# Holding eight output stores behind later loads in a fused retention and feed-forward kernel

## The chip, the cores and the metric

The kernel runs on one core of a Trainium2 chip. The metric is the device time of one execution in microseconds; smaller is better. The core has five engines with instruction queues of their own: TensorE (PE in the profile; PEld is its loading of weights), VectorE (DVE), ScalarE (ACT), GpSimd (POOL, called Pool here) and SyncE (SP). SyncE computes nothing here: it issues DMA transfers, in the order of its queue. An instruction that waits holds up everything behind it on its engine. The transfers themselves run on 16 DMA engines that all queues share.

## The reference

For 8 batches and 8 heads, with 576 positions and a head dimension of 64, retention is computed, and its output, as a matrix `x` of 4608 tokens by 512, goes through a feed-forward layer with a cosine gate:

```python
scores = scale * np.matmul(q, k.transpose(0, 1, 3, 2))
gamma = 1.0 - 2.0 ** (-5.0 - np.arange(H, dtype=np.float32))
Dmat = np.where(rel >= 0, gamma[:, None, None] ** rel[None, :, :], 0.0)
ret = scores * Dmat[None, :, :, :]
attn_out = np.matmul(ret, v)
x = attn_out.transpose(0, 2, 1, 3).reshape(B * S, H * D)

h = x @ w_in            # 512 x 2048
g = h * np.cos(h)
out = g @ w_out         # 2048 x 512
```

Inputs and output are float32; the kernel's matmuls take bfloat16.

## The kernel before

**Two tilings.** Retention works on 36 blocks of 128 tokens (`g` in the code). The feed-forward layer works on tiles of tokens (`n`): tile 0 has 512 tokens, tiles 1 and 2 have 256 each, and tiles 3 to 9 have 512 each. The output is counted in row blocks `s` of 128 rows; tiles 0 to 2 make row blocks 0 to 7, and tile 3 begins with row block 8.

**A block's way.** `load` (line 105) issues from SyncE three DMAs for a block, `fq`, `fk` and `fv`, each into a tile of a pool with five buffers for each name. `prep` (line 131) scales q and k into `qks` and casts v into `vb`, on Pool for nearly all blocks (lines 140 and 156). `transposes` (line 164) turns `qks` into `qkT`: for blocks from 6 on this is a DMA with transpose, again on SyncE (line 167). Then TensorE computes the scores (`sc`, line 195), VectorE masks them into `ret` (line 207), and `attn_out` (line 293) makes the block's part of the tile's `xT`.

**A tile's way.** `mm1` (line 354) multiplies `xT` by `w_in` into `h`; ScalarE computes the cosine (line 373) and VectorE the gated product `gT` (line 374). What follows differs:

- Tiles 0 to 2 use `mm2` (line 376): for each row block 16 matmuls (line 382) into one PSUM tile, a copy by ScalarE into a tile `ot` (line 392), a store from SyncE (line 393), and then `feed(s)`.
- Tiles 3 to 9 use `mm2_seven` (line 527), Strassen's scheme with seven products (line 517) in the order 3, 4, 5, 2, 1, 7, 6. Sums of parts of `gT` that the products need, `gs`, are made by VectorE and Pool (line 445); Pool makes them in pieces of 2 x 256 = 512 elements per partition, before the change and after it. Product 3 goes into a PSUM tile, and ScalarE copies it into `u22` (line 557). Product 5 then adds into the same PSUM tile, and its copy is `c12` (line 564). In the same way product 4 and product 2 share a tile, with the copy `c21` (line 569). VectorE joins the rest into `u11` and `u22` (lines 559 and 537). The four results `c12`, `c21`, `u11` and `u22` are stored by `store` (line 542), each store followed by `feed`.

**What sets the order.** The order of each engine's instructions is the order in which the Python code emits them. `feed(s)` (line 599) is called with each finished row block and emits, as far as limits counted in `s` allow, further `prep`s, transposes and `load`s. In `feed`, after row block 7, loads up to block 19 have been emitted, all of them behind the stores of the row blocks before them in SyncE's queue.

**Buffers of the output tiles.** All results, `ot` of tiles 0 to 2 and the four of the later tiles, come from one pool, `op` (line 70), with two buffers for each of its tags "a", "b", "c" and "d". Row block `s` takes tag `"oabcd"[1 + s % 4]`, so row blocks 0 to 3 and 4 to 7 fill all eight buffers. `u22` takes tag "a", `u11` "b", `c12` "c" and `c21` "d". A tile that takes a used buffer waits until the store that reads that buffer is complete; the waits are put in by the framework.

Of the kernel before, what the change touches and what calls it, by code (L numbers as in the profile page):

```python
# [17 lines left out]
def kernel(  # L18
# [38 lines left out]
    S7 = 3  # L57
# [106 lines left out]
    def transposes(g, banks=None, only=(0, 1)):  # L164
        qks, vb, qkT, qT = tiles["a", g]
        if g >= N_PE_T:
            nc.sync.dma_start(qkT, qks.rearrange("s m h d -> s (m h d)"), transpose=True)  # L167
            return
        for m in only:
            ps = psum.tile([P, HG, P], BF16, tag=banks[m], name="tr")  # L170
            for hg in range(HG):
                nc.tensor.transpose(
                    ps[:, hg, :],
                    qks[:, m, 2 * hg : 2 * hg + 2, :].rearrange("s h d -> s (h d)"),
                    ident,
                )
            nc.scalar.copy(qkT[:, m * HG : (m + 1) * HG, :], ps)
        if ("fv", g) in tiles and g != 3:
            nc.scalar.copy(vb, tiles.pop(("fv", g)))
# [196 lines left out]
    def mm2(n, tsi, et):  # L376
        gT = tiles["g", n]
        if et == 0:
            bank = {0: "nmnm", 1: "nm", 2: "mn"}[n][tsi]
            tiles["o", tsi] = psum.tile([P, DM], F32, tag=bank, name="o")  # L380
        ps = tiles["o", tsi]
        nc.tensor.matmul(  # L382
            ps,
            lhsT=gT[:, et, tsi * P : (tsi + 1) * P],
            rhs=w_out_sb[:, et, :],
            start=(et == 0),
            stop=(et == ET - 1),
        )
        if et == ET - 1:
            s = starts[n] // P + tsi  # L390
            ot = op.tile([P, DM], F32, tag="oabcd"[1 + s % 4], name="ot")
            nc.scalar.copy(ot, ps)  # L392
            nc.sync.dma_start(out[s * P : (s + 1) * P, :], ot)
            feed(s)

    E2 = ET // 2
    N2 = DM // 2
# [93 lines left out]
    def product(n, x):  # L491

        gT = tiles["g", n]
        parts = [(j, 0, N2) for j in range(2)]
        if x in (3, 4, 7) or (x == 1 and n < last):
            ps = psum.tile([P, 2, N2], F32, tag={3: "n", 4: "st", 1: "n", 7: "st"}[x], name="o")
            tiles["o", x] = [ps[:, j] for j in range(2)]
            tiles["all", x] = ps
        elif x == 1:
            ps = psum.tile([P, N2], F32, tag="n", name="o")  # L500
            pt = psum.tile([P, 2, 512], F32, tag="a", name="o")
            tiles["o", x] = [ps] + [pt[:, k, : N2 // 2] for k in range(2)]
        if x in (1, 6) and n == last:
            parts = [(0, 0, N2), (1, 0, N2 // 2), (1, N2 // 2, N2)]
        dst = tiles["o", {5: 3, 2: 4, 6: 1}.get(x, x)]
        lhs = {3: gT[:, :E2, :256], 4: gT[:, E2:, 256:]}.get(x)
        if lhs is None:
            lhs = tiles["gs", n, x]
        rhs = {5: w_quarter(1, 1), 2: w_quarter(0, 0)}.get(x)
        if rhs is None:  # L510
            rhs = w_sum[x]
        order = [(e, i) for e in range(E2) for i in range(len(parts))]
        if len(parts) > 2:
            order.sort(key=lambda u: u[1])
        for e, i in order:
            j, c0, c1 = parts[i]
            nc.tensor.matmul(  # L517
                dst[i],
                lhsT=lhs[:, e, j * P : (j + 1) * P],
                rhs=rhs[:, e, c0:c1],  # L520
                start=(x in (3, 4, 1, 7) and e == 0 and (i == 0 or len(parts) > 2)),
                stop=(e == E2 - 1 and (i == len(parts) - 1 or len(parts) > 2)),
                skip_group_check=True,
            )
        return parts

    def mm2_seven(n, at):

        s0 = starts[n] // P
        pend = []  # L530

        def flush():
            while pend:
                pend.pop(0)()

        def add(out_, in0, in1, op_=ALU.add):
            pend.append(lambda: nc.vector.tensor_tensor(out=out_, in0=in0, in1=in1, op=op_))  # L537

        def new(tag):
            return op.tile([P, 2, N2], F32, tag=tag, name="ot")  # L540

        def store(t, r, c, s):
            r0 = starts[n] + r * 256
            nc.sync.dma_start(
                out[r0 : r0 + 256, c * N2 : (c + 1) * N2].rearrange("(j p) c -> p j c", p=P), t
            )
            feed(s)

        for x in (3, 4, 5, 2, 1, 7, 6):
            if x in at:  # L550
                at[x](flush, pend)
            else:
                flush()
            parts = product(n, x)
            if x == 3:
                u22 = new("a")
                nc.scalar.copy(u22, tiles["all", 3])
            elif x == 4:
                pend.insert(0, lambda: nc.vector.tensor_tensor(
                    out=u22, in0=tiles["all", 4], in1=u22, op=ALU.add  # L560
                ))
            elif x == 5:
                c12, u11 = new("c"), new("b")
                nc.scalar.copy(c12, tiles["all", 3])  # L564
                add(u11, u22, tiles["all", 3], ALU.subtract)
                store(c12, 0, 1, s0)
            elif x == 2:
                c21 = new("d")
                nc.scalar.copy(c21, tiles["all", 4])  # L569
                add(u22, u22, tiles["all", 4], ALU.subtract)  # L570
                store(c21, 1, 0, s0 + 1)
            elif x == 1 and n < last:
                add(u11, tiles["all", 1], u11)
            elif x == 1:
                for (j, c0, c1), ps in zip(parts, tiles["o", 1]):
                    add(u11[:, j, c0:c1], ps, u11[:, j, c0:c1])
            elif x == 7:
                add(u11, tiles["all", 7], u11)
                flush()
                store(u11, 0, 0, s0 + 2)  # L580
            elif n < last:
                add(u22, tiles["all", 1], u22)
                flush()
                store(u22, 1, 1, s0 + 3)
            else:
                for (j, c0, c1), ps in zip(parts, tiles["o", 1]):
                    add(u22[:, j, c0:c1], ps, u22[:, j, c0:c1])
                    flush()
                    r0 = starts[n] + 256 + j * P
                    nc.sync.dma_start(out[r0 : r0 + P, N2 + c0 : N2 + c1], u22[:, j, c0:c1])  # L590
# [3 lines left out]
    def prep_next(**kw):  # L594
        nonlocal prepared
        prep(prepared, **kw)
        prepared += 1

    def feed(s):

        nonlocal loaded, prepared, transposed
        before = loaded
        n, r = divmod(s - starts[S7] // P, 4)
        if n >= 0:
            while prepared < min(NG, starts[S7] // P + 10 + 4 * n + ((0, 1, 2, 4) if n else (-1, 0, 1, 4))[r]):
                prep_next()
            while transposed < prepared:
                transposes(transposed)
                transposed += 1
            ahead = starts[S7] // P + 14 if n == 0 and r < 3 else prepared + LD  # L610
            while loaded < min(NG, prepared + LD, ahead):
                load(loaded)
                loaded += 1
            return
        while True:
            while prepared < min(loaded, 2 * s + 7, s + 11, starts[S7] // P + 8):
                prep(prepared)
                prepared += 1
                if transposed < N_PE_T:
                    transposed += 1  # L620

            if N_PE_T <= transposed < min(prepared, s + 11) and (
                transposed <= loaded - 2 or loaded == NG or (s > 3 and loaded == before)
            ):
                transposes(transposed)
                transposed += 1
            elif loaded < min(NG, 2 * s + 8, s + 13):
                load(loaded)
                loaded += 1
            else:  # L630
                break
# [148 lines left out]
    for n, w in enumerate(widths):  # L780
# [68 lines left out]
        for i, (tsi, et) in enumerate(order):  # L849
            while todo and todo[0][0] <= i:  # L850
                todo.pop(0)[1]()
            mm2(n, tsi, et)
# [31 lines left out]
```

## Time and profile before

| what | us |
|---|---|
| median of three runs (least, greatest) | 300.19 (299.92, 301.33) |
| the profiled execution's own time | 299.92 |
| its span, first to last instruction | 298.2 |
| TensorE busy | 287.1 |
| Pool busy | 209.4 |
| VectorE busy | 207.9 |
| ScalarE busy | 135.9 |
| store to landing, least / median / greatest | 1.6 / 3.6 / 5.8 |

The span is divided by the profile into what each engine did. TensorE is busy for 96% of it. The DMA engines are busy for nine tenths or more of nearly every slice up to 210 us, at some 200 GB/s, most of it in packets of under 512 bytes, which are the rows of 64 floats of q, k and v. Tile 0's first matmuls of `mm1` start at 17.9 us, tile 1's at 49.2, tile 2's at 67.5, tile 3's at 84.2, tile 4's at 116.8 and tile 5's at 149.8. The eight stores of line 393 are issued by SyncE at 41.04, 51.44, 62.31, 72.91, 84.74, 96.66, 105.38 and 109.62 us. The copies that fill them were made by ScalarE between 39.0 and 85.0 us.

A line of the timeline gives start and length in microseconds, the engine (SPq is the part of SyncE that issues DMAs), the line of the code, the operation, what is written and read, and how many are merged into the line. Brackets give the idle time before it and what ended that.

### The profile page before, as it was taken

How to read it: one execution, taken by the hardware profiler on the slowest of the kernel's cores; microseconds unless marked ns; L12 is line 12 of the kernel's file. 1: busy time of each engine (PE TensorE's matmuls, PEld its weight loads, DVE VectorE, ACT ScalarE, POOL GpSimd, SP SyncE). 2: the span in 40 equal slices, each digit the busy share in tenths (PEclk: the TensorE clock that was granted, in tenths of full speed). 3: DMA queues.
4: the chain of work that ended last, by engine and by line, in shares of the span. 5: the costliest groups of instructions: out<-in, count | busy, mean ns of one | idle time of the engine just before them, and what ended most of it. 6: DMA issues, size and time to landing. Idle time of an engine off the chain costs nothing.

```text
span 298.2 us, 7384 instructions
## 1 busy us (share of the span) xinstructions
PE 287.1 (96%) x3113; PEld 195.3 (65%) x3113; DVE 207.9 (70%) x245; ACT 135.9 (46%) x167; POOL 209.4 (70%) x214
## 2 busy tenths in 40 slices
PE   8899999999999999979999999999999999999995
PEld 3478646848578786448744875488448845874584
DVE  5677637564579994788848874887489757935872
ACT  2656433514255432642346554546464446425620
POOL 2750066436445599997999999599959946980693
PEclk9999999999999999999999999999999999999999
DMA  7999999999999999999999997998690260031013
GB/s 203 212 209 206 209 214 213 200 243 208 208 174 222 211 239 213 217 279 176 198 224 229 209 200 183 212 208 201 122 194 2 73 143 0 2 106 36 0 44 99
DMA packets 154304, 50.28 MB, mean 169 GB/s; under 512 B 140832, under 2 KB 153248, under 8 KB 154272
## 3 DMA queue, kind: packets, MB, share of 16 engines
q1 hardware_dynamic: 149504, 45.10, 77.2%
q0 software_dynamic: 4224, 4.19, 8.5%
q8 instruction: 24, 0.39, 0.6%
q10 hardware_dynamic: 544, 0.52, 0.5%
q14 instruction: 8, 0.07, 0.1%
HBM read 36.70 MB, written 9.44 MB: 155 GB/s over the span
## 4 chain that ended last, share of the span: by engine, by line
PE 43%; POOL 25%; SPq 13%; DMA 8%; DVE 5%; issue 3%; ACT 1%; POOLq 0%; DVEq 0%
PE h L365 22%; POOL gs L445 17%; PE o L517 11%; SPq L117 8%; POOL qks L140 6%; PE o L382 5%; SPq L167 4%; DVE gT L374 3%; DMA fk<-in_k_dram 2%; DMA w_in_sb<-in_moe_w_in_dram 2%; DMA qkT<-qks 2%; POOL vb L156 2%; DVE gs L445 2%; DMA fv<-in_v_dram 1%; ACT cosh L373 1%
## 5 line engine op out<-in xcount | busy, mean ns | idle before, releaser
L445 POOL TENSOR_TENSOR gs<-gT 128x512 bf16<-128x512 bf16 x102 | 116.3, 1180 | 29.4 <-DVE gs L445 29.4
L365 PE MATMUL h<-xT,w_in_sb 128*128 128x512 bf16 (+2 forms) x832 | 127.6, 313 | 2.6 <-DVE gT L374 1.8
L374 DVE TENSOR_TENSOR gT<-h,cosh 128x1024 bf16<-128x1024 f32 x72 | 87.8, 1223 | 43.7 <-ACT cosh L373 40.7
L373 ACT ACTIVATE cosh<-h,half_pi 128x1024 f32<-128x1024 f32 x72 | 80.2, 1114 | 72.2 <-PE h L365 69.8
L365 PEld LDWEIGHTS <-w_in_sb 128*128 128x128 bf16 x832 | 75.9, 98 | 51.6 <-issue 3.0
L140 POOL TENSOR_TENSOR qks<-fq,gq 128x512 bf16<-128x512 f32 x32 | 34.0, 1062 | 40.9 <-DMA fq<-in_q_dram 40.9
L517 PEld LDWEIGHTS <-gs 128*128 128x128 bf16 x576 | 53.6, 98 | 10.1 <-POOL gs L445 2.9
L140 POOL TENSOR_TENSOR qks<-fk,gk 128x512 bf16<-128x512 f32 x35 | 37.3, 1066 | 8.0 <-DMA fk<-in_k_dram 7.4
L207 DVE TENSOR_TENSOR ret<-sc,tri 128x1024 bf16<-128x1024 f32 x32 | 38.1, 1217 | 2.8 <-PE sc L195 2.7
L517 PE MATMUL o<-ws,gs 128*128 128x256 bf16 (+1 forms) x352 | 39.1, 268 | 0.7 <-POOL gs L445 0.5
L382 PE MATMUL o<-w_out_sb,gT 128*128 128x512 bf16 x128 | 30.1, 380 | 0.0
L517 PE MATMUL o<-w_out_sb,gT 128*128 128x256 bf16 x224 | 26.6, 273 | 0.1
L517 PE MATMUL o<-w_out_sb,gs 128*128 128x256 bf16 x224 | 26.1, 273 | 0.5 <-POOL gs L445 0.4
L537 DVE TENSOR_TENSOR ot<-o,ot 128x512 f32<-128x512 f32 (+2 forms) x25 | 14.9, 603 | 14.7 <-PE o L517 14.5
L517 PEld LDWEIGHTS <-gT 128*128 128x128 bf16 x224 | 21.4, 98 | 4.7 <-DVE gT L374 0.7
L350 ACT CAST xT<-ov 128x1024 bf16<-128x1024 f32 (+1 forms) x18 | 16.5, 917 | 16.1 <-PE ov L319 13.9
L445 DVE TENSOR_TENSOR gs<-gT 128x1024 bf16<-128x1024 bf16 (+1 forms) x18 | 20.4, 1148 | 0.3
L382 PEld LDWEIGHTS <-gT 128*128 128x128 bf16 x128 | 11.8, 98 | 12.5
L156 POOL CAST vb<-fv 128x512 bf16<-128x512 f32 x22 | 14.3, 651 | 4.4 <-DMA fv<-in_v_dram 4.2
L564 ACT COPY ot<-o 128x512 f32<-128x512 f32 x7 | 4.1, 586 | 20.5 <-PE o L517 20.5
L392 ACT COPY ot<-o 128x512 f32<-128x512 f32 x8 | 4.7, 588 | 17.4 <-PE o L382 17.4
L537 DVE TENSOR_TENSOR ot<-ot,o 128x512 f32<-128x512 f32 x14 | 9.6, 684 | 4.0 <-ACT ot L569 2.4
(70 smaller groups left out, 175.8 us busy)
## 6 DMA issues: line engine op xcount, KB each, us to landing
out_dram<-ot SPq DMA_DIRECT2D x35, 256.0 KB, 4.0
fk<-in_k_dram SPq DMA_DIRECT2D x32, 256.0 KB, 5.2
fv<-in_v_dram SPq DMA_DIRECT2D x32, 256.0 KB, 5.2
fq<-in_q_dram SPq DMA_DIRECT2D x30, 256.0 KB, 4.5
w_in_sb<-in_moe_w_in_dram POOLq DMA_DIRECT2D x4, 512.0 KB, 8.9
w_out_sb<-in_moe_w_out_dram POOLq DMA_DIRECT2D x4, 512.0 KB, 16.2
fq<-in_q_dram SPq DMA_DIRECT2D x8, 128.0 KB, 4.0
fk<-in_k_dram SPq DMA_DIRECT2D x8, 128.0 KB, 4.4
```

Of the source, the lines that this page charges most:

```text
L117: i = nc.sync.dma_start(f[p0:p1], src[b, :, s0 : s0 + p1 - p0, :].rearrange("h s d -> s h d"))
L140: eng.tensor_tensor(out=qks[:, m].rearrange("p (b a) d -> p a b d", a=2), in0=f.rearrange("p (a b) d -> p a b d", a=2), in1=by[:, c, :].re ...
L156: copy_v(vb, fv)
L207: nc.vector.tensor_tensor(out=ret.rearrange("p a b i -> p (a b) i"), in0=ps.rearrange("p a b i -> p (a b) i"), in1=mask.unsqueeze(1).to_br ...
L350: evac(tiles["x", n][:, :, t0 : t0 + len(gs) * P], ps.rearrange("p c x i -> p c (x i)"))
L365: nc.tensor.matmul(ps[:, j, :], lhsT=w_in_sb[:, dg, (et + j) * P : (et + j + 1) * P], rhs=xT[:, dg, c0 : c0 + w], start=(dg == 0), stop=(d ...
L373: nc.scalar.activation(cosh, ps, ACTF.Sin, bias=half_pi, scale=1.0)
L374: nc.vector.tensor_mul(gT[:, et : et + m, c0 : c0 + w], ps, cosh)
L382: nc.tensor.matmul(ps, lhsT=gT[:, et, tsi * P : (tsi + 1) * P], rhs=w_out_sb[:, et, :], start=(et == 0), stop=(et == ET - 1),)
L445: i = (nc.vector if on_dve else nc.gpsimd).tensor_tensor(out=tiles["gs", n, x][:, e : e + step], in0=i0, in1=i1, op=op_)
L517: nc.tensor.matmul(dst[i], lhsT=lhs[:, e, j * P : (j + 1) * P], rhs=rhs[:, e, c0:c1], start=(x in (3, 4, 1, 7) and e == 0 and (i == 0 or l ...
L537: pend.append(lambda: nc.vector.tensor_tensor(out=out_, in0=in0, in1=in1, op=op_))
```

## The change

In tiles 0 to 2 the store is no longer issued with its row block: the row block's tile is put on a list, `held`. After the `feed` of row block 7, behind all loads that this call and earlier ones emitted, the stores of row blocks 0 to 3 are issued. The stores of row blocks 4 to 7 follow one by one, each behind the `feed` that follows one of tile 3's four stores. The number of stores and their bytes are the same, and nothing is computed differently.

```diff
@@ mm2 @@
             s = starts[n] // P + tsi
             ot = op.tile([P, DM], F32, tag="oabcd"[1 + s % 4], name="ot")
             nc.scalar.copy(ot, ps)
+            held.append((s, ot))
+            feed(s)
+            if s == 7:
+                store_held(4)
+
+    held = []
+
+    def store_held(k):
+        for s, ot in held[:k]:
             nc.sync.dma_start(out[s * P : (s + 1) * P, :], ot)
-            feed(s)
+        del held[:k]
@@ mm2_seven, store @@
                 out[r0 : r0 + 256, c * N2 : (c + 1) * N2].rearrange("(j p) c -> p j c", p=P), t
             )
             feed(s)
+            if n == S7:
+                store_held(1)
```

## The prediction

> **What bounds the kernel now.** I read the page's busy row first (TensorE busy 96% of the span), then the timeline of TensorE over 48 to 180 us, then the timelines of ScalarE and of SyncE's DMA queue over the same time. The busy row says that the end moves only if TensorE is made to wait or stops waiting. These TensorE lines (start, length, line, operation, count; in brackets the idle time before and what ended it) are the passage that the change can reach:
>
> ```profile
> 99.55 4.12 PE L517 MATMUL o<-w_out_sb,gT 128*128 128x256 bf16 x32
> 103.59 0.64 PE L195 MATMUL sc<-qkT 64*64 64x128 bf16 x32
> 104.17 3.67 PE L517 MATMUL o<-w_out_sb,gs 128*128 128x256 bf16 x32
> ...
> 108.28 0.32 PE L266 MATMUL st<-v_odd,qks 128*64 128x64 bf16 x8 [0.45 <-POOL gs L445]
> ...
> 130.81 1.89 PE L365 MATMUL h<-xT,w_in_sb 128*128 128x512 bf16 x8 [1.78 <-DVE gT L374]
> ```
>
> The first line is products 3 and 4 of tile 3, the second the scores of blocks 12 and 13, the third products 5 and 2. There is no gap between them, so every microsecond by which product 5 starts after 104.17 is a microsecond of TensorE. Behind it two gaps, 0.45 and 1.78 us, could be given back. What product 5 needs is on ScalarE:
>
> ```profile
> 101.49 0.59 ACT L557 COPY ot<-o 128x512 f32<-128x512 f32 x1 [0.58 <-PE o L517]
> 106.12 0.59 ACT L564 COPY ot<-o 128x512 f32<-128x512 f32 x1 [4.05 <-PE o L517]
> ```
>
> The first is the copy of product 3 into `u22`. Product 5 adds into the same PSUM tile, so it can't begin before this copy has read it. Now the SyncE queue, which issues in order:
>
> ```profile
> 41.04 1.13 SPq L393 DMA_DIRECT2D out_dram<-ot  x1
> 42.22 0.43 SPq L117 DMA_DIRECT2D fq<-in_q_dram  x1
> ...
> 84.74 0.57 SPq L393 DMA_DIRECT2D out_dram<-ot  x1
> 86.39 1.47 SPq L167 DMA_TRANSPOSE qkT<-qks  x1
> ...
> 96.66 0.53 SPq L393 DMA_DIRECT2D out_dram<-ot  x1
> 98.04 1.25 SPq L167 DMA_TRANSPOSE qkT<-qks  x1
> ...
> 105.38 1.08 SPq L393 DMA_DIRECT2D out_dram<-ot  x1
> 106.50 0.43 SPq L117 DMA_DIRECT2D fq<-in_q_dram  x1
> ...
> 109.62 0.89 SPq L393 DMA_DIRECT2D out_dram<-ot  x1
> 110.56 0.43 SPq L117 DMA_DIRECT2D fq<-in_q_dram  x1
> 111.03 2.27 SPq L117 DMA_DIRECT2D fk<-in_k_dram  x1
> 113.35 1.61 SPq L117 DMA_DIRECT2D fv<-in_v_dram  x1
> 115.06 0.88 SPq L544 DMA_DIRECT2D out_dram<-ot  x1
> ```
>
> The reader is to see how late SyncE runs. Row block 7 was copied by ScalarE at 84.38, and its store is issued at 109.62; tile 2's last load, block 19, is issued at 113.35 to 114.96, and tile 3's first store at 115.06. TensorE is by then 11 us into tile 3's products. From 31.8 to 115 us the queue has hardly a hole, and the page's second part shows DMA at 9 in every slice of it.
>
> **What the Trainium skill says.** "Perfetto Trace Analysis", What "DMA-bound" means: an issuing queue that is solid DMA slices is itself a bound. The trace agrees, with the gaps above (1.08 us ahead of 86.39, 0.85 ahead of 98.04) where a transpose waits for Pool instead. "TensorE: Matmul & The Clock Gate", Part 1: after an idle window of about 3.4 us the array runs at half rate until about 3.4 us of activity have passed. The trace shows the slow start only at the program's beginning: the 14 warm-up matmuls of 128x512 take 5.32 us, 380 ns each, against 13.98 us for 64 such ones at 149.83, 218 ns each; the granted clock reads 1.00 in both. "SBUF — State Buffer", Who interferes with whom: a VectorE instruction with two SBUF inputs and a GpSimd instruction that reads SBUF exclude each other. The trace agrees: the VectorE sum of 128x1024 at 126.30 takes 3.33 us while Pool works without a break, and 0.69 us at 135.14; behind it stands the 1.78 us gap.
>
> **The change part by part.**
>
> *Eight stores leave the load stream.* Each removed store gives SyncE back the time to the next issue: 1.18 us for row block 0 (41.04 to 42.22), 0.58 each for 1, 2 and 3 (the same reading at 51.44, 62.31, 72.91), 1.12 for 6, 0.94 for 7. Blocks 4 and 5 give nothing there, because the transpose behind them waits for Pool's scaling anyway. The sum is 1.18 + 3 x 0.58 + 1.12 + 0.94 = 5.0 us. Counted in DMA time it is the same: between 258 and 262 us one store runs alone with a DMA share of 0.19 over 4 us, 0.76 us; eight are 6.1 us, and since the shares in this stretch add up to 1.24 they are worth about 4.9 us of it. What do earlier loads buy? TensorE's only gap before 103 us in this stretch, 0.69 us at 67.49, waits for VectorE's `xT` copy, not for a load. So this part is worth nothing at the end by itself (bounds: 0 to 0.5 us gain; I take 0).
>
> *Four stores behind tile 2's loads.* They take the place where tile 3's first store stood, 115.06, less the 5.0 us: row block 0 is issued at about 110.1. Bounds: 107.5 if all eight count fully and landings quicken too, 112 if the waits for Pool eat most of it. A store's landing takes 1.6, 3.6 or 5.8 us (least, median, most of all stores); behind a full queue of loads I take 4.2. It lands at 114.3.
>
> *The new wait.* `u22` of tile 3 is the third tile of tag "a", which has two buffers; in the changed program it gets row block 0's, and the copy at L557 waits for that store. In the kernel before, that store was issued at 41.04 and cost nothing; now it lands at 114.3, and the copy, wanted at 101.49, ends at 114.3 + 0.59 = 114.9. With about 0.1 us to TensorE, product 5 starts at 115.0 instead of 104.17: 10.8 us of standing still. Queued behind the copy on ScalarE are the copies of `c12` and `c21` and the next `xT`; on VectorE the sum L559, which needs `u22`, with the masks of blocks 12 and 13 behind it. All of these feed TensorE work later than product 5, and keep their distance to it. Row blocks 1, 2 and 3 land up to some 3 us after block 0; `c12`, which waits for block 2, is wanted 2 us after product 5's start, so this stays about level. Bounds of the stall: 107.5 + 3.6 + 0.7 - 104.2 = 7.6 us and 112 + 5.8 + 0.7 - 104.2 = 14.3 us.
>
> *Half rate after the stall.* The trace of before has no long idle time of TensorE in its middle, so this is bounded: 0, or half of 3.4 us up to all of it if the window is met badly. An estimate from the skill's clock page: 3.4 us at half rate lose 1.7 us. I take 1.7 (0 to 3.4).
>
> *What is given back.* The 0.45 us gap is put down to Pool's sums (104.76 to 111.46), which will be done by then; it may rather be VectorE's sum at 107.47 to 108.14, which frees the PSUM bank that the next matmuls write, and VectorE, 0.43 us behind TensorE at L559 before, starts level with it after the stall. In either reading the gap goes. Pool's scaling of blocks 17 to 21 (116.25 to 129.07) depends on loads 20 and 21, which SyncE may issue only after tile 3's first store; that store waits for `c12`, ready about 117.7 instead of being issued at 115.06. Loads 20 and 21 come some 3 us later than before, Pool is free by about 131, and VectorE's sum comes at 126.30 + 10 = 136 without Pool beside it: the 1.78 us gap goes. The later gaps (0.46, 0.27 and 0.40 us at 147, 149 and 172) follow TensorE's own pace and stay. Given back: 2.2 us (0 to 3.4).
>
> *Four stores with tile 3's.* One each behind its four stores, 0.5 to 1.1 us of SyncE each, in a stretch where loads for tile 5 follow. Pool needs those from 149 us on, now about 159, so 3 to 4 us of delay are covered; if that cover of 6 us were gone, each microsecond would show. Row block 7's store comes only behind loads 22 to 26, at about 156. Tile 4's `d` tile does not wait for it: in the changed program's waits it takes the buffer of tile 3's `c21`, stored at about 126. Cost 0.
>
> *Sum.* 10.8 + 1.7 - 2.2 = +10.3 us. From 180 to 249 us TensorE runs without gaps at 29.4 us per tile, so nothing more comes back. The profiled execution took 299.92 us (span 298.2 and 1.7 around it): 310.2. The median of the runs is 300.19, 0.27 higher: **310.5 us**.
>
> **The rivals.**
>
> *A short stall (0.17).* The stream gains as much as the lower bound says, with quick landings: 7.6 us, no half rate, 3.4 us given back: +4.2, 304.4 us. For it: DMA-saturated slices; against: the waits for Pool at 86.39 and 98.04.
>
> *A second wait (0.14).* SyncE stands from about 113 to 117.7 for `c12`, and loads 20 to 22 slip by more than the 6 us of cover, so Pool's sums of tile 4 come late: 6 to 8 us on top, about 317. For it: Pool is busy almost without holes from 104 to 185 us; against: its waits there are for VectorE, not for loads.
>
> *No stall, not slower (0.05).* Loads, Pool and transposes form a chain in which one waits for the other; if each removed store shortened it by more than its own time, row block 0 would land before product 5 wants it. That takes an issue by about 100 us, so 15 us gained, 1.9 us per store against the 0.62 counted here. From there on the time is 299.9 to 300.2, or up to 2 us less if the gaps close too. That the copy doesn't wait at all, because `u22` takes another buffer, would end the same way; the changed program's waits speak against it.
>
> **How the numbers follow.** The likeliest case holds 0.64: 310.5 us, its own range 307 to 314.5. Down to 305 takes in most of the short stall, up to 316 part of the second wait: 305 to 316 leaves out about 2 in 10. 0.5% (1.5 us) is about what a measurement can tell from no change. Slower: 0.64 + 0.17 + 0.14 = 0.95; the last case splits into same 0.03 and faster 0.02.
>
> **What would show it.** In the changed profile: ScalarE's copy of `u22` waits about 12 us, ended by the DMA out_dram; TensorE has one gap of about 11 us ahead of the products of `gs` near 104; the first matmuls after it take up to twice their 115 ns for 128x256; the four stores stand together near 110 to 113 in SyncE's queue; no gap ahead of tile 4's last h matmuls. I am wrong if the four stores are issued before 101 us, or if a gap of some microseconds stands anywhere else after 130 us.

## The result and the profile after

The changed kernel takes 311.24 us (310.99 to 312.31, four runs) against 300.06 us for the kernel before on the same chip: ratio 1.0371, 95% interval 1.0332 to 1.0411. The forecast was 310.5 us. The profiled execution has a span of 309.3 us, 11.1 more than before.

In the view of all waits, the new one has these lines (who waited for whom: us in total, times, longest):

```profile
ACT ot L568 <- DMA out_dram<-ot: 15.5, 1, 15.5
...
PE o L526 <- ACT ot L568: 12.7, 1, 12.7
DVE ot L570 <- ACT ot L568: 12.5, 1, 12.5
```

One wait of ScalarE for a store, 15.5 us long, and behind it one wait each of TensorE and VectorE for ScalarE. No other line of this view is a wait for a store (`out_dram<-ot`). In the timelines of SyncE's DMA queue, of ScalarE and of TensorE the same wait has its place:

```profile
110.52 1.15 SPq L117 DMA_DIRECT2D fv<-in_v_dram  x1
111.72 2.61 SPq L402 DMA_DIRECT2D out_dram<-ot  x4
120.68 0.38 SPq L553 DMA_DIRECT2D out_dram<-ot  x1
```

```profile
99.54 1.12 ACT L373 ACTIVATE cosh<-h,half_pi 128x1024 f32<-128x1024 f32 x1 [0.69 <-PE h L365]
116.15 0.59 ACT L568 COPY ot<-o 128x512 f32<-128x512 f32 x1 [15.49 <-DMA out_dram<-ot]
120.06 0.59 ACT L575 COPY ot<-o 128x512 f32<-128x512 f32 x1 [3.33 <-PE o L526]
```

```profile
99.34 4.19 PE L526 MATMUL o<-w_out_sb,gT 128*128 128x256 bf16 x32
103.46 0.64 PE L195 MATMUL sc<-qkT 64*64 64x128 bf16 x32
116.78 4.99 PE L526 MATMUL o<-w_out_sb,gs 128*128 128x256 bf16 x32 [12.69 <-ACT ot L568]
121.70 0.32 PE L266 MATMUL st<-v_odd,qks 128*64 128x64 bf16 x8
...
129.80 13.98 PE L365 MATMUL h<-xT,w_in_sb 128*128 128x512 bf16 x64
143.61 3.66 PE L526 MATMUL o<-w_out_sb,gT 128*128 128x256 bf16 x32
...
160.46 0.61 PE L526 MATMUL o<-ws,gs 128*128 128x256 bf16 x4 [0.27 <-POOL gs L454]
```

SyncE issues the four held stores from 111.72 us, straight behind block 19's last load. The copy into `u22`, now on line 568, starts at 116.15, when the first of them has landed; before, it started at 101.49. Product 5 starts at 116.78 instead of 104.17. SyncE then stands until the copy of `c12` is made, and issues its store at 120.68. The lines from 143.61 us on show what was given back: no gap stands in front of tile 4's products, and the small gap before 160.46 is the one that the kernel before has here:

```profile
149.38 0.61 PE L517 MATMUL o<-ws,gs 128*128 128x256 bf16 x4 [0.27 <-POOL gs L445]
```

The view of stretches gives TensorE's granted clock (the column behind POOL's count) after the stall; its columns are the stretch, its length, busy time and count of PE, PEld, DVE, ACT and POOL, the clock, the DMA share and GB/s:

```profile
105.00:110.00 5.00, 0.00 (x0) 0.00 (x0) 0.00 (x0) 0.00 (x0) 5.00 (x6) 0.93 1.29 220
110.00:115.00 5.00, 0.00 (x0) 0.00 (x0) 0.00 (x0) 0.00 (x0) 5.00 (x6) 0.50 1.31 231
115.00:118.00 3.00, 1.22 (x6) 0.86 (x6) 1.23 (x2) 0.59 (x1) 3.00 (x4) 0.50 0.75 289
118.00:120.00 2.00, 2.00 (x14) 1.51 (x12) 1.72 (x2) 0.00 (x0) 2.00 (x3) 0.61 0.00 0
120.00:125.00 5.00, 5.00 (x113) 4.29 (x111) 3.46 (x6) 2.79 (x5) 3.50 (x5) 1.00 0.81 100
```

The clock falls to 0.50 while TensorE stands and is back at 1.00 in the stretch from 120 us. Products 5 and 2 run in between: 4.99 us, against 3.67 before.

The shift of TensorE against the kernel before, read from these lines and those of before:

| event | before | after | shift |
|---|---|---|---|
| product 5 starts | 104.17 | 116.78 | 12.61 |
| tile 4's h begins | 116.78 | 129.80 | 13.02 |
| tile 4's products begin | 132.53 | 143.61 | 11.08 |
| tile 5's h begins | 149.83 | 160.91 | 11.08 |
| span | 298.2 | 309.3 | 11.1 |

So 12.61 us of later start, and 4.99 - 3.67 = 1.32 us of half rate, make 13.93. Up to tile 4's h 0.91 us of that is gained back (13.93 - 13.02), and 1.94 within tile 4, where the gap of 1.78 us is gone. What is left, 11.08 us, stays to the end.

### The profile page after: what moved, and what is told of

Its sections match the earlier page's. It is cut to its first block, busy times and chain, and to the rows that moved or that the text cites. A ratio compares the mean times of both kernels' runs of the same rounds, so it can differ in the third digit from the quotient of the medians.

```text
span 309.3 us, 7382 instructions
## 1 busy us (share of the span) xinstructions
PE 288.3 (93%) x3113; PEld 196.2 (63%) x3113; DVE 205.6 (66%) x245; ACT 135.8 (44%) x167; POOL 209.4 (68%) x214
## 4 chain that ended last, share of the span: by engine, by line
PE 48%; POOL 28%; DMA 9%; SPq 7%; issue 4%; DVE 1%; POOLq 0%; ACT 0%; DVEq 0%
PE h L365 24%; POOL gs L454 19%; PE o L526 11%; PE o L382 7%; POOL qks L140 7%; SPq L117 6%; DMA fk<-in_k_dram 4%; DMA fq<-in_q_dram 4%; PE sc L195 2%; DMA fv<-in_v_dram 1%; POOL vb L156 1%; PE ov L333 1%; PE ov L319 1%; SPq L167 1%; PE st L266 1%
## 5 line engine op out<-in xcount | busy, mean ns | idle before, releaser
L526 PEld LDWEIGHTS <-gs 128*128 128x128 bf16 x576 | 54.4, 99 | 23.1 <-issue 13.0
L526 PE MATMUL o<-w_out_sb,gs 128*128 128x256 bf16 x224 | 27.4, 281 | 13.2 <-ACT ot L568 12.7
L454 DVE TENSOR_TENSOR gs<-gT 128x1024 bf16<-128x1024 bf16 (+1 forms) x18 | 17.0, 957 | 0.3
L570 DVE TENSOR_TENSOR ot<-o,ot 128x512 f32<-128x512 f32 x7 | 4.8, 685 | 13.3 <-ACT ot L568 12.5
L575 ACT COPY ot<-o 128x512 f32<-128x512 f32 x7 | 4.1, 586 | 19.8 <-PE o L526 19.8
```

The lines of the kernel that those rows point to most:

```text
L454: i = (nc.vector if on_dve else nc.gpsimd).tensor_tensor(out=tiles["gs", n, x][:, e : e + step], in0=i0, in1=i1, op=op_)
L526: nc.tensor.matmul(dst[i], lhsT=lhs[:, e, j * P : (j + 1) * P], rhs=rhs[:, e, c0:c1], start=(x in (3, 4, 1, 7) and e == 0 and (i == 0 or l ...
```

## The experiments

**Is it the wait for the store's landing, or SyncE's queue?** Four kernels, e1 to e4, ask this; the kernel before ran beside them at 299.95 us. In e1 the held stores are left out:

```diff
-            nc.sync.dma_start(out[s * P : (s + 1) * P, :], ot)
+            pass
```

> The changed kernel with the eight held stores left out: row blocks 0 to 7 of the output are never written, so this run shows what the load stream does without these stores and what tile 3 does without a store to wait for. Theory (the time is lost by the copy into u22, which waits for row block 0's store): no stall at product 5, 299.9 us, within 0.7 of the kernel before; block 19's last load still ends near 111.7 us as in the changed kernel, because the loads gain little. Rival (the loss comes from TensorE's stall alone, but earlier loads are worth something that the stall hides): 297 to 298.5 us. Rival (the loss comes from SyncE's queue, in which loads 20 and 21 stand behind the held stores): near 300 us too, so this run doesn't tell it apart; the next three do.

Measured: 299.65 us, ratio 0.9988 (0.9976 to 0.9999). Product 5 starts at 103.92, without a gap, and the copy into `u22` waits only for TensorE:

```profile
103.92 3.67 PE L526 MATMUL o<-w_out_sb,gs 128*128 128x256 bf16 x32
```

```profile
101.45 0.59 ACT L568 COPY ot<-o 128x512 f32<-128x512 f32 x1 [0.63 <-PE o L526]
```

Block 19's last load ends its issue at 110.04, 4.9 us earlier than in the kernel before; it was expected at 111.7. The medians differ by 0.3 us: earlier loads alone buy next to nothing.

The next two, e2 and e3, move the four stores forward in SyncE's queue by one and by two blocks' loads (in e3 the condition is `s == 6`):

```diff
-            feed(s)
             if s == 7:
                 store_held(4)
+            feed(s)
```

> Stores of row blocks 0 to 3 issued ahead of row block 7's feed, so that block 19's three loads stand behind them instead of before them; all else as in the changed kernel. Theory: row block 0's store is issued at about 108.0 instead of 111.7 us, lands near 112.3, product 5 starts near 113.1: the stall shrinks from 12.7 to 9.0 us and the time from 311.2 to 307.5 us. Rival (SyncE's queue and the loads behind it): block 19 to 21 are loaded later, not earlier, so 311 to 312 us.

> The same, with the four stores ahead of row block 6's feed: the loads of blocks 18 and 19 stand behind them. Theory: issue at about 104.5, landing near 108.8, product 5 near 109.6: stall 5.5 us, 304.0 us, a little less if TensorE comes back before it falls to half rate. Rival (SyncE's queue): 311 to 313 us.

Measured: 307.93 us (ratio 1.0256, 1.022 to 1.0292) and 303.69 us (1.0119, 1.0081 to 1.0157). The TensorE line of product 5 in each:

```profile
113.47 5.48 PE L526 MATMUL o<-w_out_sb,gs 128*128 128x256 bf16 x32 [9.20 <-ACT ot L568]
```

```profile
109.84 5.05 PE L526 MATMUL o<-w_out_sb,gs 128*128 128x256 bf16 x32 [5.56 <-ACT ot L568]
```

Here the store's place in the queue is the dose and the stall the response:

| kernel | store of row block 0 issued | copy into u22 starts | product 5 starts | TensorE stood | time |
|---|---|---|---|---|---|
| two loads earlier | 104.72 | 109.20 | 109.84 | 5.56 | 303.69 |
| one load earlier | 108.25 | 112.83 | 113.47 | 9.20 | 307.93 |
| as changed | 111.72 | 116.15 | 116.78 | 12.69 | 311.24 |

From the issue of the store to product 5 it takes 5.1 to 5.2 us in all three, and each microsecond of earlier issue is about a microsecond of time. The loads of blocks 18 and 19 are later in the two experiments than in the changed kernel; if they had set the time, it would have risen. Loads 20 and 21 come earlier, not later as the rival had it: load 20 is issued at 119.52 and 117.12 us instead of 122.50, because tile 3's first store, which waits for `c12`, stands ahead of it and `c12` is ready sooner. But in e3 it is issued even before that of the kernel before (118.13), and the time is still 3.7 us longer. The rival on SyncE's queue falls.

In e4, row block 0 is stored at once and only 1 to 7 are held:

```diff
             held.append((s, ot))
+            if s == 0:
+                store_held(1)
             feed(s)
             if s == 7:
-                store_held(4)
+                store_held(3)
```

> Only row block 0 is stored at once, as before; row blocks 1 to 7 are held as in the changed kernel. Theory: u22 gets its buffer in time and product 5 starts at 104.2, but the copy into c12 waits for row block 2's store, which lands near 116.5, and the next matmuls that use its PSUM bank start near 117.9 instead of 108.3: a stall of 9.6 us in a new place, with half rate behind it, and 309 us. Rival (it is row block 0's store alone): 300 to 301 us. Rival (SyncE's queue): 311 us.

Measured: 309.04 us, ratio 1.0302 (1.0276 to 1.0327). TensorE and ScalarE:

```profile
103.51 3.67 PE L528 MATMUL o<-w_out_sb,gs 128*128 128x256 bf16 x32
118.02 0.43 PE L266 MATMUL st<-v_odd,qks 128*64 128x64 bf16 x8 [10.83 <-DVE ot L548]
```

```profile
101.16 0.59 ACT L570 COPY ot<-o 128x512 f32<-128x512 f32 x1 [0.63 <-PE o L528]
116.56 0.58 ACT L577 COPY ot<-o 128x512 f32<-128x512 f32 x1 [14.82 <-DMA out_dram<-ot]
```

Product 5 is on time, at 103.51. The copy of `c12` waits for row block 2's store, and the next matmuls into its PSUM bank start after a gap of 10.83 us. The wait isn't the first store's own: take it away, and the next tile that needs a held store's buffer stops TensorE 3 us later, at 107.18 instead of 104.10.

**The four stores that go with tile 3's.** In e5 only row blocks 4 to 7 are held; the kernel before ran beside it at 299.92 us:

```diff
             held.append((s, ot))
+            if s < 4:
+                store_held(1)
             feed(s)
-            if s == 7:
-                store_held(4)
```

> Row blocks 0 to 3 are stored at once, as before; only row blocks 4 to 7 are held, one behind each store of tile 3. Theory (a held store costs only where a tile of tile 3 waits for it, and these four are first waited for in tiles 4 and 5, long after they land): no stall, within 0.7 us of the kernel before, 299.3 to 300.7 us, although SyncE's queue carries four more stores ahead of tile 5's loads. Rival (stores among tile 3's transposes and tile 5's loads delay Pool): 302 to 305 us.

Measured: 301.19 us, ratio 1.0045 (1.0022 to 1.0067): slower by about 1.3 us, nearly twice the expected bound, and less than the rival said. TensorE's timeline has two gaps that the kernel before has not:

```profile
168.29 0.42 PE L195 MATMUL sc<-qkT 64*64 64x128 bf16 x16 [0.72 <-DMA qkT<-qks]
...
175.63 0.42 PE L195 MATMUL sc<-qkT 64*64 64x128 bf16 x16 [0.23 <-DMA qkT<-qks]
```

They are waits for transposes, 0.95 us together, ahead of scores in tile 5. (A third one, of 0.98 us at 83.08, stands ahead of the first store that is held; e7, e10 and e11 below, which hold none, have it too, with 0.94, 0.70 and 0.61 us.) SyncE issues tile 5's loads from 136.1 us instead of 133.5, because four more stores stand before them or among them, and the transposes behind come late. Tile 5 takes 0.76 us more in this profile (from 150.46 to 181.23, against 149.83 to 179.84); the rest of the difference arose ahead of it. So these four stores cost about 1 us when TensorE isn't late itself. In the changed kernel, where it is 11 us late, no such gap is seen.

**The half rate.** Fifty (e6) or 62 (e9) matmuls of 128x512 on zeros go into the stall:

```diff
-    5: lambda then, off: (then(), scores2(g)),
+    5: lambda then, off: (then(), scores2(g), keep_warm(n)),
...
+    def keep_warm(n):
+        if n == S7:
+            warm(psum.tile([P, 512], F32, tag="m", name="idle"), 50)
```

> The changed kernel, with 50 matmuls of 128x512 on zeros into a free PSUM bank between the scores and product 5, so that TensorE works through most of the stall. Theory (after the stall TensorE runs at half rate for about 3 us and loses 1.3 us): the granted clock stays at 1.00, products 5 and 2 take 3.7 us instead of 5.0, and the time is 309.9 us against 311.2. Rival (the slower products 5 and 2 come from VectorE and ScalarE starting late after the stall): 311 us and 5.0 us again.

> As e6_warm_in_stall, with 62 matmuls on zeros instead of 50: about 13.4 us, so that TensorE stands still for less than 1 us before product 5. In e6 it stood for 2.8 us and still fell to half rate. Theory (the slower products 5 and 2 are the half rate): granted clock 1.00 throughout, products 5 and 2 in 3.7 us, and 1.3 us less than the changed kernel if the last matmul on zeros ends before the copy, 309.9 to 310.9 us. Rival (VectorE and ScalarE starting late): 5 us for the two products again.

With 50: 311.39 us, ratio 1.0358 (1.0317 to 1.0399). The store happened to be issued at 112.79, so that TensorE still stood for 2.83 us before product 5, and this was enough for half rate. The four runs differ: two with a mean granted clock of 0.992 took 312.14 and 312.47 us, two with 0.998 and 1.00 took 309.16 and 310.64. With 62: 311.27 us, ratio 1.0388 (1.0363 to 1.0413), beside a kernel before of 299.69. (The profile of this one has records of 60 of the 62.) The product lines and the stretches after the stall, first for 50:

```profile
103.75 10.96 PE L185 MATMUL idle<-zeros 128*128 128x512 bf16 x50
117.55 5.32 PE L526 MATMUL o<-w_out_sb,gs 128*128 128x256 bf16 x32 [2.83 <-ACT ot L568]
```

```profile
115.00:118.00 3.00, 0.46 (x4) 0.41 (x4) 0.47 (x1) 0.58 (x1) 3.00 (x4) 0.98 0.93 343
118.00:120.00 2.00, 2.00 (x12) 1.39 (x11) 2.00 (x3) 0.00 (x0) 2.00 (x3) 0.50 0.01 5
```

and for 62:

```profile
104.35 13.33 PE L185 MATMUL idle<-zeros 128*128 128x512 bf16 x60 [0.16 <-issue]
117.52 3.66 PE L526 MATMUL o<-w_out_sb,gs 128*128 128x256 bf16 x32
```

```profile
115.00:118.00 3.00, 2.95 (x17) 1.54 (x17) 1.57 (x2) 0.59 (x1) 3.00 (x4) 1.00 0.49 186
118.00:120.00 2.00, 2.00 (x21) 1.79 (x19) 1.38 (x2) 0.54 (x1) 2.00 (x3) 1.00 0.00 0
```

In the second the clock stays at 1.00 and the two products take 3.66 us, though VectorE and ScalarE start nearly as late as in the changed kernel (the copy at 115.81 instead of 116.15). The half rate's share, 1.3 us in the products, is thereby shown. The time did not fall with it: the matmuls on zeros ran until about 117.5, 1.1 us past the end of the copy at 116.40. When tile 4's h began, 0.60 us of the 1.3 were left (129.20 against 129.80), and the spans are equal, 309.3 us. What the half rate costs at the end of the kernel is not shown by this run.

**Why the loads gained little.** Who held up SyncE's queue between 40 and 112 us is told by these lines, first of the kernel before, then of the changed one (us in total, times, longest):

```profile
SPq L167 <- POOL vb L156: 2.6, 2, 1.4
SPq L167 <- POOL qks L140: 1.3, 2, 0.8
```

```profile
SPq L167 <- POOL qks L140: 10.4, 5, 3.0
...
SPq L167 <- POOL vb L156: 1.2, 1, 1.2
```

The stores are gone from this stretch, and the transposes' waits for Pool have grown from 3.9 to 11.6 us. This is more than the chance of two executions: they sum to 3.8 to 6.9 us in the four profiles with the eight stores in their old places (the kernel before, e7, e10, e11), and to 8.4 to 11.6 in the six with all eight put off to the end of this stretch or left out (the changed kernel, e1, e2, e3, e6, e9). What it cost the queue is less than these sums. Before, the eight stores with the idle time ahead of them took 6.5 us of SyncE's timeline; after, the transposes with the idle time ahead of them take 26.9 us instead of 24.4, and the loads 0.5 us more.

The experiment e8 moves transposes one load later, by one condition in `feed`; it reaches those of blocks 6 to 11, one less than its expectation says:

```diff
-                transposed <= loaded - 2 or loaded == NG or (s > 3 and loaded == before)
+                transposed <= loaded - 3 or loaded == NG or (s > 3 and loaded == before)
```

> The changed kernel, with the transposes of blocks 6 to 12 each one load later in SyncE's queue. It asks why the loads gained 3.3 us and not 5.0. Theory (a load, Pool's scaling, the transpose and the next load form a loop, so SyncE stands at the transposes and the time of a removed store goes into that): block 13's load is issued at 75 us or earlier, against 79.0, though the time may rise by some us, because scores then wait for their transposes. Rival (the DMA engines are the limit in this stretch): block 13's load at 78 to 80 us, as in the changed kernel.

Measured, in a single run: 311.8 us. Block 13's load is issued at 76.00 us, between the two expectations; the waits for Pool in the same stretch fall to 6.8 us. But the held stores are issued at 111.76, as in the changed kernel, because the queue stands again at the transposes of blocks 12 to 15, which kept their place, and TensorE has two new gaps, 1.42 us before 63.25 and 1.26 before 85.15, for transposes that come late. The run does not decide between the two expectations: with no transpose moved, the same load is issued at 76.08 us in e1 and between 76.61 and 78.46 in e9, e6, e3 and e2, so the 79.00 of the changed kernel's profile is no measure for it. The loop of load, scaling and transpose fits the grown waits, but it is not shown to set the pace; this is left open.

**Can the gap at 129 us be had without the stall?** The changed kernel had shown this gap of 1.78 us to be removable. A first attempt on the kernel before, e7, was meant to make tile 4's first group of sums one h block later:

```diff
-        elif n == S7 + 1 and i in (3, 7):
+        elif n == S7 + 1 and i in (4, 7):
             for x in (5, 2, 1):
-                g_sum(n, x, i - 3, i + 1)
+                g_sum(n, x, 4 * (i // 7), 4 * (i // 7) + 4)
```

> The kernel before, with tile 4's first group of sums (for products 5, 2 and 1, first half) emitted one h block later, so that VectorE's sum doesn't run beside Pool's scaling of blocks 19 to 21. Theory (the gap of 1.78 us at 129 us comes from this sum, which took 3.33 us while Pool was busy, and not from VectorE's load as such): the sum takes about 1 us, the gap is gone, Pool's sums still end in time, and the time falls by 1.3 to 1.8 us to about 298.4, ratio 0.995. Rival (the gap is VectorE's own load, moved along): no change, 300.0 us.

Measured: 308.4 us, ratio 1.0285 (1.0264 to 1.0305). The edit did something else: at `i == 3` the branch of the later tiles now took over, made the first half of all five sums; three of them were made again after the next block and the other two after the last. The trace has 24 pieces of sums on Pool in tile 4 instead of 16, in one row:

```profile
130.55 27.63 POOL L445 TENSOR_TENSOR gs<-gT 128x512 bf16<-128x512 bf16 x24 [0.63 <-DVE gs L445]
```

As an accident it is a measurement, though not a clean one: eight pieces of 1.15 us are 9.2 us of Pool, and the kernel lost 8.5. TensorE waits 2.11, 0.50 and 2.29 us for Pool's sums, and behind these waits its granted clock is 0.50 from 145 to 150 us, so part of the loss is half rate. The edit that was meant is e10:

```diff
-        elif n == S7 + 1 and i in (3, 7):
-            for x in (5, 2, 1):
-                g_sum(n, x, i - 3, i + 1)
+        elif n == S7 + 1:
+            for x in (5, 2, 1) if i in (5, 7) else ():
+                g_sum(n, x, 0 if i == 5 else 4, 4 if i == 5 else E2)
```

> What e7_sum_later was meant to be: in e7 the first group of sums was made a block earlier by the branch for later tiles and then once more, so Pool had 12 pieces too many. Here the kernel before has tile 4's first group of sums (products 5, 2 and 1, first half) two h blocks later and once only. Theory (the gap of 1.78 us at 129 us comes from VectorE's sum held up by Pool's scaling): the sum takes 0.7 to 1.2 us, the gap is gone and Pool is still in time, 298.3 us, ratio 0.994. Rival (the gap is VectorE's own load, or the later start of Pool's sums gives it back at the second group): 300 us or more.

Measured: 299.82 us, ratio 0.9999 (0.9987 to 1.0011). (The surplus in the run before it is eight pieces, not the twelve of this expectation.) VectorE's sum takes 0.68 us instead of 3.33, and the gap before tile 4's last h matmuls is gone. Pool and TensorE:

```profile
131.00 18.30 POOL L445 TENSOR_TENSOR gs<-gT 128x512 bf16<-128x512 bf16 x16 [1.13 <-DVE gs L445]
```

```profile
143.79 0.61 PE L517 MATMUL o<-ws,gs 128*128 128x256 bf16 x4 [0.50 <-POOL gs L445]
144.90 0.61 PE L517 MATMUL o<-ws,gs 128*128 128x256 bf16 x4 [0.50 <-POOL gs L445]
...
149.35 0.61 PE L517 MATMUL o<-ws,gs 128*128 128x256 bf16 x4 [0.28 <-POOL gs L445]
```

Pool's sums now run without a break, but end at 149.3 as before, and TensorE's waits for them end at 143.79, 144.90 and 149.35 us. The gap was real; what stood behind it was Pool's row. The rival's second half holds. Therefore e11 takes two casts of v from Pool, again in the kernel before:

```diff
-            copy_v = nc.scalar.copy if g > starts[S7] // P + 17 else nc.gpsimd.tensor_copy
+            copy_v = nc.scalar.copy if g > starts[S7] // P + 17 or g in (17, 18) else nc.gpsimd.tensor_copy
```

> The kernel before, with the casts of v of blocks 17 and 18 on ScalarE instead of Pool. After e10_sum_two_later the theory is that in tile 4 the bound is Pool's row of work from 105 to 149 us: in e10 the gap of 1.76 us went and came back as waits for Pool's sums, whose last ended at 149.2 us as before. Two casts of 0.56 us less on Pool then let VectorE's sum end about 1.1 us earlier and Pool's last sum of tile 4 too: 298.9 us, ratio 0.996. Rival (it is VectorE's or TensorE's row that sets the end of tile 4, or ScalarE waits for the loads of v): 300 us or more.

Measured: 299.1 us against 299.9 of the kernel before, ratio 0.9981 (0.9962 to 1.0). VectorE's sum takes 0.83 us, the gap is gone, and Pool's last sum of tile 4 ends at 148.4; TensorE's wait for it ends at 148.50 instead of 149.38, though tile 4's h began 1.1 us later in this profile (117.86):

```profile
127.37 0.83 DVE L445 TENSOR_TENSOR gs<-gT 128x1024 bf16<-128x1024 bf16 x1
```

```profile
148.50 0.61 PE L517 MATMUL o<-ws,gs 128*128 128x256 bf16 x4 [0.28 <-POOL gs L445]
```

So the trace shows tile 4 shorter. Of the kernels that write the whole output this one has the lowest median, 0.8 us below the kernel before; but its interval just touches no change, so that a gain of the whole kernel is not shown.

## Why the prediction was right

**The new wait** carried it, and the runs show it. The step "the copy at L557 waits for that store" has the place and the engine right: e1 takes the store away and the stall goes, e2 and e3 move the store and the stall moves with it, e4 keeps the first store out of it and the stall moves to the next buffer. The sign "waits about 12 us" was too small even for the forecast's own landing at 114.3: ScalarE was free from 100.91 us on in the kernel before (99.79 plus 1.12), 13.4 us ahead of it. It waited 15.49 us.

**The stall's size** was forecast as 10.8 us and was 12.6. The term that was off is "each removed store gives SyncE back the time to the next issue", 5.0 us in sum. In the changed kernel the held stores stand at 111.72 us where tile 3's first store stood at 115.06: 3.3 us were gained. Part of the freed time went into the transposes, which wait for Pool. The prediction had reckoned with this for row blocks 4 and 5 only; its bound, an issue at 112 us "if the waits for Pool eat most of it", is nearly what came. The gain also differs from one execution to the next. The first store behind block 19's loads is issued at 115.06, 115.42, 116.06 and 116.59 us with the eight stores in their old places (the kernel before, e7, e11, e10), and at 110.14, 111.66, 111.72 and 112.79 without (e1, e9, the changed kernel, e6). The medians of the two rows are 4.0 us apart, so over these profiles the term was about 1 us too large. The landing, taken as 4.2 us, was 4.4 (111.72 to 116.15).

**Half rate** was taken as 1.7 us out of 0 to 3.4 and was 1.32. The cause is shown by e9, where the clock stayed up and the two products took 3.66 us. The size varies: after their stalls the same products took 5.48 us in e2, 5.05 in e3 and 5.32 in e6, so the loss lies between 1.3 and 1.8 us.

**What is given back** was taken as 2.2 us and was 2.85 (13.93 - 11.08). The 1.78 us gap went for the reason given: VectorE's sum took 0.69 us instead of 3.33, with Pool idle beside it. The sum before and after, and Pool's first sums of tile 4 after:

```profile
126.30 3.33 DVE L445 TENSOR_TENSOR gs<-gT 128x1024 bf16<-128x1024 bf16 x1
```

```profile
139.31 0.69 DVE L454 TENSOR_TENSOR gs<-gT 128x1024 bf16<-128x1024 bf16 x1
```

```profile
140.08 4.49 POOL L454 TENSOR_TENSOR gs<-gT 128x512 bf16<-128x512 bf16 x4 [5.18 <-DVE gs L454]
```

e10 adds what the prediction didn't see: without the stall, closing the same gap by a later sum isn't worth anything, because Pool's row stands behind it. The stall had given Pool time.

**Earlier loads** by themselves were put at 0, with a bound of 0.5 us; e1 has 0.3. **Loads 20 and 21** came 4.4 us later (122.50 against 118.13), not 3, and Pool was done with them at 134.9, not 131. It was still 4.4 us ahead of VectorE's sum.

**Four stores with tile 3's** were put at 0 with a cover named for it. e5 speaks for the cover: without the stall they cost about 1 us, with it no gap of theirs is left. The store of row block 7 was issued at 162.13, not 156, and ScalarE's copy of `c21` in tile 4, at 151.47, did not wait for it, as said.

The terms' errors have both signs, +1.8 for the stall, -0.4 for the half rate and -0.65 for what is given back, and add up to 0.8 us. That the total came so near is in part luck, since one term alone was off by more than twice as much. The rival of a short stall would have needed the issue at 107.5; that of a second wait has no line in the trace.

## What to carry to other kernels

A store that is put off holds its buffer for as long. Before moving one behind other transfers, look for the next tile that takes the buffer, read when it is wanted and when the queue will have reached the store, and compare: the difference, not the store's own cost, is the price. In an in-order queue the gap left by a removed transfer isn't a gain by itself: look at what the instruction behind it waits for. A gap on the busiest engine is worth its length only if the engine that feeds it has as much to spare.

## What was not expected of the hardware

In e6 TensorE stood for 2.83 us only, between 114.7 and 117.55, and still ran products 5 and 2 at half rate: 5.32 us, with a granted clock of 0.50 from 118 to 120 us. In e9, where it stood for next to nothing, they took 3.66 us. "TensorE: Matmul & The Clock Gate", Part 1, of the Trainium skill gives an idle window of about 3.4 us; here less was enough. In this run the clock fell only about 0.3 us after TensorE had begun to work again.

Nor is the time from the last matmul to the fall a fixed one. It can be read from the granted clock in stretches of half a microsecond to one. In e2 TensorE stops at 104.27 us and the clock reads 0.50 from 107.0 on, 2.7 us later; in e4 the fall comes 3.9 us after the stop, in e3 5.0 us and in the changed kernel 5.2 us.

Taking stores of 256 KB out of a stretch in which DMA looked full did not raise the rate there. From 40 to 50 us it was 220 to 223 GB/s in the four profiles with the eight stores in place and 192 to 207 in the six without. Block 12's load, behind four of the stores, was issued at 73.45 us instead of 73.49 in the pair of kernels compared, and at 71.24 to 72.94 in e1, e2, e3, e6 and e9, where the old place of the stores gave 73.94 to 74.52 in e7, e10 and e11.
